# QKV weight slices 0 and 1 in row halves on two DMA queues, in a fused attention and SwiGLU kernel

## The chip, the cores and the metric

The kernel runs on one core of a Trainium2 chip. The metric is the device time of one execution in microseconds (us); the figure given is the median over runs.

## The reference

All tensors are bfloat16. One layer norm of `x` feeds two branches, and both are added to `x`: a local, dilated attention (32 heads of 18, each position sees 8 positions at distance 0, 2, ..., 14 before it) and a SwiGLU block.

```python
x = A_x                                   # (1, 2048, 576)
xn = _layernorm(x)
return x + _A_ref(xn, A_wqkv, A_wo) + _B_ref(xn, B_w_gate, B_w_up, B_w_down)

def _A_ref(x, wqkv, wo):                  # wqkv (576, 1728), wo (576, 576)
    q, k, v = split_heads(x @ wqkv)       # H = 32, Dh = 18
    idx = pos[:, None] - 2 * arange(8)    # masked where idx < 0
    attn = softmax(q . k[idx] * Dh ** -0.5)
    return merge_heads(attn . v[idx]) @ wo

def _B_ref(x, w_gate, w_up, w_down):      # (576, 4608), (576, 4608), (4608, 576)
    return (silu(x @ w_gate) * (x @ w_up)) @ w_down
```

## The kernel before

The 2048 positions are cut into 16 "rows" of 128: position `16 p + r` lies in partition `p` of row `r`, so each partition of an x load reads consecutive bytes. The width of 576 makes five slices of the contraction: `kt` 0 to 3 of 128 each, and `kt` 4 of 64, which is laid in both halves of the partitions.

**Loads at the start (lines 144 to 165).** A DMA is issued by an engine's queue: `nc.sync` is SyncE's, `nc.scalar` ScalarE's. `load_x(eng, j)` brings one x row (144 KB) into `xc_b[0]`, `load_w(eng, kt)` one slice of the QKV weights (432 KB; slice 4 as two transfers of 64 partitions and 108 KB). The order is written out by hand: ScalarE issues x row 0 and slice 1; SyncE issues x row 1, slice 0, slice 2, x row 2, slice 3, slice 4, x row 3, and then x rows 4 to 15 in three transfers of four rows (576 KB each). The x buffers lie in the tile `wd`, the QKV weights in the tile `hT`, both of which get their real contents later; in the profile their transfers are called so. Every transfer tells of its landing through one of eight counters, taken in turn over both queues.

**Start of the computation (lines 477 to 523).** TensorE first runs products of constants (`warm_pe`). Row 0 is centred on VectorE as soon as its statistics are there, transposed on TensorE (`transp_pe`, L262), copied by ScalarE into `xcT` (L268, in the tile `PP`) in three pieces, and multiplied with the QKV slices in the order 0, 1, 2 (`p_whole`, L301, four products of 432 columns for each slice); the division by the standard deviation follows when the result is copied out (`p_evac`). Row 1 is normalized meanwhile (L240, its 64 columns of padding on GpSimd, L243), transposed between the products of slice 2, and its products with slice 0 stand ahead of row 0's with slice 3 and slice 4 (`p_row0_rest`). The weights' loads are waited for by the first product that reads them.

**The rest.** Rows 1 to 15 go through `p_row`, in products of 64 by 128 that run in pairs; from row 5 on x is transposed by DMA. The statistics of two rows (`ln_stats`, L214) are taken about four rows ahead; those of rows 8 and 9 while TensorE is at row 4. Keys and values go through `stage` buffers in `hT` into a ring of rows, and to DRAM (`store`, L384) for later. Then four passes over 512 positions each follow: nine chunks of gate and up products (`g_pair`, L600) and the down and output products (`d_half`, L629). The chunk weights (`load_gu`) of chunk `it + 2` are issued when chunk `it` is done. VectorE and ScalarE do the attention beside TensorE, in portions that `dve.pump` lets out. In the first pass, after chunk 0, the values of the last four rows are written to DRAM in three pieces (`store(2, 3, 3)`).

Of the kernel before, what the change touches and what calls it, by code (L numbers as in the profile page):

```python
# [17 lines left out]
P = 128  # L18
H, DH, W, DIL = 32, 18, 8, 2
D = H * DH  # L20
# [50 lines left out]
def kernel(  # L71
# [11 lines left out]
    nc = tc.nc  # L83
# [6 lines left out]
    x_v = A_x.rearrange("b (p r) d -> p (b r) d", r=R)  # L90
# [31 lines left out]
    wdf = wd[:].rearrange("p f j -> p (f j)")  # L122
    XC, XN = RT * D, RT * DPAD
    xc_b = [wdf[:, i * XC:(i + 1) * XC].rearrange("p (r d) -> p r d", d=D) for i in range(4)]
# [4 lines left out]
    wqkv = hTf[:, 0:12 * D].rearrange("p (k j) -> p k j", j=3 * D)  # L129
# [14 lines left out]
    def load_x(eng, j):  # L144
        eng.dma_start(xc_b[0][:, j:j + 1, :], x_v[:, j:j + 1, :])  # L145

    def load_w(eng, kt):
        if kt < 4:
            eng.dma_start(wqkv[:, kt, :], A_wqkv[kt * P:(kt + 1) * P, :])
        else:  # L150
            for i in range(2):
                eng.dma_start(wqkvr[64 * i:64 * i + 64, :], A_wqkv[4 * P:D, 2 * G * i:2 * G * (i + 1)])

    load_x(nc.scalar, 0)
    load_x(nc.sync, 1)
    load_w(nc.scalar, 1)
    load_w(nc.sync, 0)
    make_identity(nc, ident[:])
    load_w(nc.sync, 2)
    load_x(nc.sync, 2)  # L160
    load_w(nc.sync, 3)
    load_w(nc.sync, 4)
    load_x(nc.sync, 3)
    for c in range(1, 4):
        nc.sync.dma_start(xc_b[c], x_v[:, 4 * c:4 * c + 4, :])
    nc.scalar.activation(warm[:], eps_t[:], ACT.Sqrt)

    wp = ps.tile([P, 512], f32, name="warm_ps", tag="ps")
# [10 lines left out]
    def load_gu(it):  # L179
        ch, slot = it % NCH, it % NSLOT  # L180
        fc = slice(ch * FC * P, (ch + 1) * FC * P)
        nc.sync.dma_start(gu[:, slot, 0:4, :], B_w_gate[0:512, fc].rearrange("(kt kp) n -> kp kt n", kp=P))
        nc.sync.dma_start(gu[:, slot, 4:8, :], B_w_up[0:512, fc].rearrange("(kt kp) n -> kp kt n", kp=P))
        nc.sync.dma_start(gu[0:64, slot, 8, :], B_w_gate[512:576, fc])
        nc.sync.dma_start(gu[64:128, slot, 8, :], B_w_up[512:576, fc])

    def load_wo(d):
        k, row = divmod(d * H, P)
        for lo in (row, row + 64) if k == KT - 1 else (row,):
            nc.sync.dma_start(wo[lo:lo + H, k, :], A_wo.rearrange("(h d) j -> d h j", d=DH)[d])  # L190

    def load_wd(ch):
        nc.sync.dma_start(wd[:, ch * FC:(ch + 1) * FC, :],
                          B_w_down[ch * FC * P:(ch + 1) * FC * P, :].rearrange("(f p) j -> p f j", p=P))
# [185 lines left out]
    def store(m, c, parts=1):  # L380
        st = stage[(2 * c + m - 1) % 4].rearrange("p r d -> p (r d)")
        n = XC // parts
        for i in range(0, XC, n):
            nc.sync.dma_start(kv_d[m - 1, c - 1, :, i:i + n], st[:, i:i + n])  # L384
# [197 lines left out]
    def g_pair(tt, ch, p):  # L582


        slot = (tt * NCH + ch) % NSLOT
        tok = slice(tt * TT, (tt + 1) * TT)
        js = (2 * p, 2 * p + 1)
        fence = {}
        for j in js:
            ring_ps[j] = [new_ps("g_ps") for b in range(2)]  # L590
        for swap in range(2):
            for j in js:
                fc = slice(j * P, (j + 1) * P)
                kts = (0, 1, 2, 3) if swap else (0, 4, 1, 2, 3)
                for kt in kts:
                    for half in range(2):
                        b = half ^ swap
                        rows = slice(64 * half, 64 * half + 64)
                        k = 8 if kt == 4 else 4 * b + kt
                        mm = nc.tensor.matmul(ring_ps[j][b][:], gu[rows, slot, k, fc], xnT[rows, kt, tok],  # L600
                                              start=(swap == 0 and kt == 0), stop=(swap == 1 and kt == 3))
                        if swap == 0 and kt == 3 and half == 1:
                            fence[j] = fence_after(mm)
                        if swap and kt == 0 and half == 0:
                            fence_before(mm, fence[j])

    def g_evac(ch, j):
        t = ring_ps[j]
        sg = tmp.tile([P, TT], bf16, name="sg", tag="sg", bufs=3)
        uc = tmp.tile([P, TT], bf16, name="uc", tag="uc", bufs=3)  # L610
        nc.scalar.activation(sg[:], t[0][:], ACT.Silu)  # L611
        nc.scalar.copy(uc[:], t[1][:])  # L612
        nc.vector.tensor_tensor(hT[:, ch * FC + j, :], sg[:], uc[:], op=ALU.mult)  # L613

    def d_half(tt, sub, swap, t, fence):


        r = RT * tt + sub
        tiles = [(hT[:, f, sub * P:(sub + 1) * P], wd[:, f, :]) for f in range(NF)]
        tiles += [(oT[:, k, r * P:(r + 1) * P], wo[:, k, :]) for k in range(KT - swap)]  # L620
        if r == R - 1:
            tiles.insert(NF, (ident, xr[:, sub, :]))
        if not swap:
            t[sub] = [new_ps("d_ps") for h in range(2)]
        for n, (a, w) in enumerate(tiles):
            for half in range(2):
                rows = slice(64 * half, 64 * half + 64)
                h = half ^ swap
                mm = nc.tensor.matmul(t[sub][h][:, 0:HALF], a[rows], w[rows, h * HALF:(h + 1) * HALF],  # L629
                                      start=(swap == 0 and n == 0), stop=(swap == 1 and n == len(tiles) - 1))  # L630
                if not swap and n == len(tiles) - 1 and half == 1:
                    fence[sub] = fence_after(mm)
                if swap and n == 0 and half == 0:
                    fence_before(mm, fence[sub])

    def d_out(r, sub, t):
        ot = tmp.tile([P, D], bf16, name="ot", tag="ot", bufs=3)
        for h in range(2):
            cols = slice(h * HALF, (h + 1) * HALF)
            if r < R - 1:  # L640
                nc.vector.tensor_tensor(ot[:, cols], t[h][:, 0:HALF], xr[:, sub, cols], op=ALU.add)  # L641
                continue
            (nc.scalar.copy, nc.vector.tensor_copy)[h](ot[:, cols], t[h][:, 0:HALF])  # L643
        nc.sync.dma_start(out_v[:, r, :], ot[:])

    for tt in range(NTT):
        for ch in range(NCH):
            it = tt * NCH + ch
            for p in range(2):
                g_pair(tt, ch, p)  # L650
                for j in (2 * p, 2 * p + 1):
                    g_evac(ch, j)
                    if it % NCH < NCH - 1 or p == 0:
                        dve.pump(1.4)
            if ch == NCH - 1:
                dve.drain(lambda: chains[0] > tt)
                for r in range(RT * tt, RT * tt + RT):
                    nc.sync.dma_start_transpose(oT[:, :, r * P:(r + 1) * P], QOP[:, r, :])
                for i in (0, 2):
                    nc.sync.dma_start(xr[:, i:i + 2, :], x_v[:, RT * tt + i:RT * tt + i + 2, :])  # L660
            if it + NSLOT < NTT * NCH:
                load_gu(it + NSLOT)
            if tt == 0:
                if 1 <= ch <= 7:
                    load_wd(ch - 1)
                if ch in (3, 4):
                    load_wd(11 - ch)
                for _ in range(3 if ch in (1, 2) else 2):
                    if wo_order:
                        load_wo(wo_order.pop(0))  # L670
                if ch == 0:
                    store(2, 3, 3)
            if ch == 1 and tt < NTT - 1:
                chain(tt + 1)
        for sub in range(0, RT, 2):
            t, fence = {}, {}
            for swap in range(2):
                for i in (sub, sub + 1):
                    d_half(tt, i, swap, t, fence)
                    if swap:  # L680
                        dve.pump(12.5 if i == sub else 4.0)
                        d_out(RT * tt + i, i, t[i])
# [30 lines left out]
```

## Time and profile before

| | |
|---|---|
| median of 3 runs | 503.36 us (503.14 to 503.4) |
| the profiled execution | 503.32 us, its span 501.5 us |
| PE (TensorE) busy | 496.8 us, 99% |
| DVE (VectorE) / ACT (ScalarE) / POOL (GpSimd) busy | 329.0 / 200.6 / 2.6 us |
| moved by DMA | 75.42 MB, mean 150 GB/s |
| ScalarE's DMA queue (q10) | 288 packets, 0.59 MB |
| SyncE's DMA queue (q1) | 76840 packets, 73.98 MB |
| clock granted to TensorE | 1.00 |

Times in the profile are microseconds from the start of the span. An engine's name with a q (SPq, ACTq) is its issuing of instructions, PEld is TensorE's loading of the operand that stays in the array. `out<-in` names the tiles written and read; `xcount` is the number of instructions in a line, and what stands in brackets is the idle time ahead of it and what ended it. Ends of products are modelled, so a busy TensorE need not be at its peak.

### The profile page before, as it was taken

Reading aid. Unit: us, or ns where it says so; the run is one execution under the profiler, and the core shown is the slowest. Engines: PE = TensorE matmul, PEld = TensorE weight load, DVE = VectorE, ACT = ScalarE, POOL = GpSimd, SP = SyncE. Lnnn points to the kernel's source line nnn. Section 1 sums busy time; section 2 is a strip of 40 time slices with the busy share of each in tenths; the row PEclk is TensorE's granted clock in tenths of the full one; section 3 lists DMA queues with packets and bytes.
Section 4 is the critical chain, followed back from the end, with each engine's and each line's share of the span. In section 5 each row is a group of like instructions: output and inputs, shape, how many; then the busy total and the mean of one; then the engine's idle time right before and its main releaser. Section 6 shows DMA issues by size and latency. Waiting matters only on the chain.

```text
span 501.5 us, 13267 instructions
## 1 busy us (share of the span) xinstructions
PE 496.8 (99%) x5795; PEld 282.8 (56%) x5795; DVE 329.0 (66%) x478; ACT 200.6 (40%) x415; POOL 2.6 (1%) x9
## 2 busy tenths in 40 slices
PE   8999999999999999999999999999999999999997
PEld 4555544444677644444777544445777444446775
DVE  5889597998999698999897139995980222221001
ACT  4756657645300255544300445557000454553000
POOL 2000000000000000000000000000000000000000
PEclk9999999999999999999999999999999999999999
DMA  8689989898731045535631154453700335442200
GB/s 322 164 207 228 320 268 294 260 318 272 186 114 61 25 147 185 190 112 174 166 106 47 30 182 154 131 189 110 181 26 14 106 110 177 159 126 39 76 14 25
DMA packets 77186, 75.42 MB, mean 150 GB/s; under 512 B 22708, under 2 KB 72528, under 8 KB 77128
## 3 DMA queue, kind: packets, MB, share of 16 engines
q1 hardware_dynamic: 76840, 73.98, 49.2%
q8 instruction: 45, 0.74, 0.7%
q10 hardware_dynamic: 288, 0.59, 0.3%
q14 instruction: 13, 0.11, 0.1%
HBM read 58.76 MB, written 5.90 MB: 129 GB/s over the span
## 4 chain that ended last, share of the span: by engine, by line
PE 98%; DMA 1%; DVE 0%; SPq 0%; issue 0%
PE g_ps L600 56%; PE d_ps L629 32%; PE qkv_ps L301 11%; DMA hT<-in_A_wqkv_dram 1%; DVE ot L643 0%; PE pt L283 0%; SPq L145 0%; PE pt L262 0%; PE warm_ps L262 0%
## 5 line engine op out<-in xcount | busy, mean ns | idle before, releaser
L600 PE MATMUL g_ps<-xnT,gu 64*128 64x512 bf16 x2592 | 280.4, 376 | 0.0
L600 PEld LDWEIGHTS <-gu 64*128 64x128 bf16 x2592 | 126.1, 94 | 152.9
L611 ACT ACTIVATE sg<-g_ps 128x512 bf16<-128x512 f32 x144 | 87.3, 606 | 156.6 <-PE g_ps L600 156.6
L629 PE MATMUL d_ps<-wd,hT 64*128 64x288 bf16 x2304 | 146.4, 283 | 0.0
L629 PEld LDWEIGHTS <-hT 64*128 64x128 bf16 x2304 | 112.2, 94 | 29.7
L613 DVE TENSOR_TENSOR hT<-sg,uc 128x512 bf16<-128x512 bf16 x144 | 60.0, 419 | 93.9 <-ACT uc L612 93.8
L612 ACT CAST uc<-g_ps 128x512 bf16<-128x512 f32 x144 | 85.2, 592 | 0.0
L414 DVE TENSOR_REDUCE PP<-PP 128x64 f32<-128x1152 bf16 x64 | 84.9, 1346 | 0.4
L301 PE MATMUL qkv_ps<-hT,xnT 64*128 64x432 bf16 (+1 forms) x536 | 50.1, 343 | 0.0
L409 DVE TENSOR_TENSOR PP<-QO,Kr 128x2304 bf16<-128x2304 bf16 (+1 forms) x35 | 43.5, 1249 | 7.0 <-DMA Kr<-hT 6.8
L641 DVE TENSOR_TENSOR ot<-d_ps,xr 128x288 bf16<-128x288 f32 x30 | 12.3, 450 | 51.1 <-PE d_ps L629 51.1
L441 DVE TENSOR_TENSOR PP<-Vr,A 128x2304 bf16<-128x2304 bf16 (+1 forms) x35 | 43.2, 1250 | 0.4
L301 PEld LDWEIGHTS <-xnT 64*128 64x128 bf16 (+1 forms) x536 | 25.9, 94 | 22.5 <-ACT xnT L287 0.2
L446 DVE TENSOR_TENSOR PP<-PP 128x2304 bf16<-128x2304 bf16 x24 | 32.5, 1353 | 0.3
L611 ACT ACT_TABLE_LOAD x5 | 6.4, 1283 | 47.2 <-PE g_ps L600 47.2
L629 PE MATMUL d_ps<-wo,xnT 64*128 64x288 bf16 x288 | 22.9, 283 | 0.0
L363 ACT CAST hT<-qkv_ps 128x288 bf16<-128x288 f32 (+2 forms) x58 | 21.1, 427 | 0.5 <-ACT hT L363 0.5
L434 ACT ACTIVATE PP<-PP 128x1024 f32<-128x1024 f32 x4 | 4.2, 1056 | 31.2 <-DVE PP L430 31.2
L629 PEld LDWEIGHTS <-xnT 64*128 64x128 bf16 x288 | 14.0, 94 | 3.6
L643 ACT CAST ot<-d_ps 128x288 bf16<-128x288 f32 x1 | 0.4, 399 | 38.8 <-PE d_ps L629 38.8
L363 ACT CAST QO<-qkv_ps 128x432 bf16<-128x432 f32 (+1 forms) x30 | 12.3, 409 | 7.4 <-PE qkv_ps L301 7.4
L214 DVE BATCH_NORM_STATS2 stats<-wd 128x6 f32<-128x288 bf16 x32 | 12.9, 444 | 2.8 <-DMA wd<-in_A_x_dram 2.6
(53 smaller groups left out, 89.4 us busy)
## 6 DMA issues: line engine op xcount, KB each, us to landing
gu<-in_B_w_gate_dram SPq DMA_DIRECT2D x36, 512.0 KB, 3.9
gu<-in_B_w_up_dram SPq DMA_DIRECT2D x36, 512.0 KB, 5.2
wd<-in_B_w_down_dram SPq DMA_DIRECT2D x9, 576.0 KB, 6.4
kv_d<-hT SPq DMA_DIRECT2D x5, 576.0 KB, 6.0
gu<-in_B_w_gate_dram SPq DMA_DIRECT2D x36, 64.0 KB, 5.0
gu<-in_B_w_up_dram SPq DMA_DIRECT2D x36, 64.0 KB, 4.6
xr<-in_A_x_dram SPq DMA_DIRECT2D x8, 288.0 KB, 3.9
out_dram<-ot SPq DMA_DIRECT2D x16, 144.0 KB, 1.8
```

What stands on the lines that cost most here:

```text
L214: nc.vector.bn_stats(sums[r][:, k, :], xc[:, j, k * HALF:(k + 1) * HALF])
L301: return nc.tensor.matmul(t[g][:, 0:G], xT_of(r)[rows, kt, :], w_at(g, kt, rows), start=start, stop=stop)
L363: (nc.vector.tensor_copy if n in dve else nc.scalar.copy)(*parts[n])
L409: nc.vector.tensor_tensor(prod[:, a:b], QO[:, RT * tt + a:RT * tt + b, :], Kr[:, s:s + b - a, :], op=ALU.mult)
L414: nc.vector.tensor_reduce(L[:, w, rs], prod[:, rs].rearrange("p r (h d) -> p r h d", d=DH), axis=AX.X, op=ALU.add)
L441: nc.vector.tensor_tensor(dst[:, a:b], Vr[:, s:s + b - a, :].rearrange("p r (d h) -> p r d h", h=H), A[:, w, a:b].unsqueeze(2).to_broadcas ...
L446: nc.vector.tensor_tensor(dst, acc, pv, op=ALU.add)
L600: mm = nc.tensor.matmul(ring_ps[j][b][:], gu[rows, slot, k, fc], xnT[rows, kt, tok], start=(swap == 0 and kt == 0), stop=(swap == 1 and kt ...
L611: nc.scalar.activation(sg[:], t[0][:], ACT.Silu)
L612: nc.scalar.copy(uc[:], t[1][:])
L613: nc.vector.tensor_tensor(hT[:, ch * FC + j, :], sg[:], uc[:], op=ALU.mult)
L629: mm = nc.tensor.matmul(t[sub][h][:, 0:HALF], a[rows], w[rows, h * HALF:(h + 1) * HALF], start=(swap == 0 and n == 0), stop=(swap == 1 and ...
```

## The change

Slices 0 and 1 are each loaded as two transfers of 64 rows (216 KB): rows 0 to 63 on SyncE's queue, rows 64 to 127 on ScalarE's, slice 0 ahead of slice 1 on both. x rows 8 to 15 come in one transfer of 1152 KB instead of two of 576. The store of the last values goes out in two pieces of 288 KB instead of three of 192, so the number of transfers over the whole kernel stays what it was.

```diff
     load_x(nc.scalar, 0)
     load_x(nc.sync, 1)
-    load_w(nc.scalar, 1)
-    load_w(nc.sync, 0)
+    for kt in range(2):
+        for eng, lo in ((nc.scalar, 64), (nc.sync, 0)):
+            eng.dma_start(wqkv[lo:lo + 64, kt, :], A_wqkv[kt * P + lo:kt * P + lo + 64, :])
     make_identity(nc, ident[:])
     load_w(nc.sync, 2)
     load_x(nc.sync, 2)
     load_w(nc.sync, 3)
     load_w(nc.sync, 4)
     load_x(nc.sync, 3)
-    for c in range(1, 4):
-        nc.sync.dma_start(xc_b[c], x_v[:, 4 * c:4 * c + 4, :])
+    nc.sync.dma_start(xc_b[1], x_v[:, 4:8, :])
+    nc.sync.dma_start(wdf[:, 2 * XC:4 * XC].rearrange("p (r d) -> p r d", d=D), x_v[:, 8:16, :])
     nc.scalar.activation(warm[:], eps_t[:], ACT.Sqrt)
...
                 if ch == 0:
-                    store(2, 3, 3)
+                    store(2, 3, 2)
```

## The prediction

> **What bounds the kernel now.** I read first the chain that ended last in order of time, then the start of the timeline, then the windows of the first 13 us (transfer rate), and last the waits of SyncE's queue. The chain:
>
> ```profile
> 1.17 4.79 DMA hT<-in_A_wqkv_dram
> 5.97 0.04 issue
> 6.01 1.99 PE qkv_ps L301 x10
> ...
> 12.46 3.10 PE qkv_ps L301 x34
> ...
> 19.14 40.52 PE qkv_ps L301 x444
> 59.66 69.93 PE g_ps L600 x648
> 129.59 39.69 PE d_ps L629 x648
> ```
>
> From 6.01 us to the end of the products at 498.4 the chain never leaves TensorE, so a change to the loads can do one of two things: let TensorE start its first real product earlier than 6.01, or make it wait somewhere later. The start hangs on QKV slice 0, issued on SyncE's queue at 1.17 and landed at 5.97. What else the first product needs is in the timeline:
>
> ```profile
> 5.45 0.27 ACT L268 COPY PP<-pt 128x128 bf16<-128x128 bf16 x1 [0.28 <-PE pt L262]
> ...
> 5.77 1.80 PEld L301 LDWEIGHTS <-PP 128*128 128x128 bf16 x10
> 5.93 0.37 ACT L268 COPY PP<-pt 128x256 bf16<-128x256 bf16 x1 [0.21 <-PE pt L262]
> 6.01 1.99 PE L301 MATMUL qkv_ps<-hT,PP 128*128 128x432 bf16 x10
> ```
>
> The other operand, the transposed x row 0, is copied by 5.72 and is in the array from 5.77. So slice 0 holds TensorE for 6.01 - 5.77 = 0.24 us, and that is all that its earlier landing can give.
>
> The rates (columns: stretch, length, busy time of PE, PEld, DVE, ACT, POOL, then clock, DMA share, GB/s):
>
> ```profile
> 3.00:5.00 2.00, 1.53 (x7) 0.45 (x4) 1.15 (x4) 0.26 (x2) 0.06 (x1) 1.00 1.03 408
> 5.00:6.00 1.00, 0.63 (x5) 0.42 (x6) 1.00 (x4) 0.51 (x3) 0.53 (x1) 1.00 1.04 418
> 6.00:7.50 1.50, 1.49 (x9) 0.81 (x9) 1.33 (x6) 0.86 (x3) 0.96 (x2) 1.00 1.05 398
> 7.50:9.25 1.75, 1.75 (x14) 1.03 (x13) 1.02 (x4) 0.74 (x2) 0.40 (x1) 1.00 1.08 314
> 9.25:13.00 3.75, 3.75 (x46) 1.91 (x45) 3.05 (x10) 2.49 (x7) 0.00 (x0) 1.00 1.02 410
> ```
>
> From 3 us on the transfer engines are full at about 410 GB/s, except from 7.5 to 9.25, where they moved 314. What moved there is the last QKV slice, two transfers of 64 partitions each (L152, 0.22 MB together), and x row 3. That is the only row of this trace on 64-partition transfers, and the change makes four more of them.
>
> **The change part by part.** The sum is made against the profiled execution, 503.32 us: a span of 501.5 and 1.8 around it. The median of the runs is 503.36, so a difference can be laid on either.
>
> *Order of slices 0 and 1.* Before, slice 1 stood on ScalarE's queue and slice 0 on SyncE's, 0.44 MB each, and they shared the engines: the trace has them landed at 5.68 and 5.97. After, each queue has a half of slice 0 ahead of a half of slice 1, so slice 0 is whole after half of these bytes. The x rows 0 and 1 landed at 3.75 and 3.93; the two slices took 5.97 - 3.93 = 2.04 us more, half of it gives about 4.95, and at the poorest rate of the table (314 instead of 410) 5.27. Both are ahead of 5.72, so TensorE starts on its other operand: at 5.77, plus one more wait, since a product now needs two landings. The chain shows 0.04 from a landing to the product; I take 0.05, between nothing and 0.10, and a start at 5.82: a gain of 0.19 us (bounds 0.14 to 0.24).
>
> *Does it carry on?* Products of the first row run every 0.182 us. Slice 1 is due at 5.82 + 4 x 0.182 = 6.55; the copy of L268 that it needs ends at 6.30. Slice 2 is due at 6.01 + 8 x 0.182 = 7.47 before and 7.28 after; in the trace it landed at 7.14, with 0.04 to the product 7.18. Its margin shrinks from 0.29 to 0.10. Slice 3 landed at 8.84, due at 9.31 before and 9.12 after; slice 4 at 9.58, due at 10.14 and 9.95. The row 1 operand is normalized by 7.44 (VectorE) and 7.90 (its padding, GpSimd) and wanted from 7.64 and 8.17. So slice 2 is the next thing to be late, if the halves travel slower than whole slices.
>
> *Rate of the halves.* By the page of before, 1.75 us at 314 instead of 410 GB/s lose 1.75 x 96/410 = 0.41 us on 0.22 MB of lone halves, 1.86 us per MB. Not all of the new halves are alone: while ScalarE's queue sends rows 64 to 127, SyncE's sends rows 0 to 63. The two queues end apart, though: up to 4.75 us ScalarE's had moved 0.57 of its 0.59 MB, SyncE's only 0.45, so the last 0.14 MB of slice 1 go on SyncE's queue with no partner. Priced by the row of the lone halves that is 0.14 x 1.86 = 0.26 us by which everything behind comes later. The bounds are 0 (the halves pair perfectly, or the 314 came from the short rows of slice 4 and x row 3) and 0.88 x 1.86 = 1.65 us (each half as slow as a lone one). I take 0.26, since the traffic up to the point where ScalarE's queue runs empty is over all 128 partitions as in the stretch of 408. Slice 1 then lands at 6.23, in time. Slice 2 is ready at 7.18 + 0.26 = 7.44 against 7.28: TensorE waits 0.16 of its 0.19 again. Slice 3 is ready at 9.14 against 9.28, slice 4 at 9.88 against 10.11: nothing more.
>
> [...]
>
> *Issues.* An issue takes about 0.44 us on SyncE and 0.46 on ScalarE. ScalarE gets one more, which moves its table load from 1.63 to 2.09 and the end of its warm-up from 3.13 to 3.59; its next work is at 4.88, so 1.29 us of idle time cover it (0.46 without). SyncE's queue gets one more issue ahead of slice 2, and the trace shows each transfer held until the one eight places before it has landed:
>
> ```profile
> SPq L165 <- DMA hT<-in_A_wqkv_dram: 1.4, 2, 0.8
> SPq L183 <- DMA hT<-in_A_wqkv_dram: 0.9, 1, 0.9
> ```
>
> Two transfers more move these pairs: slice 3 now waits for x row 0 (3.75), slice 4 for x row 1 (3.93) and a half of slice 0 (about 4.9), x row 3 for the other half, x rows 4 to 7 for a half of slice 1 (about 6.0 instead of 5.70). Slice 3 is issued at about 3.8 instead of 2.62, slice 4 from 4.3 instead of 3.11. By then 1.76 MB are issued and some 0.6 moved, so over 2.5 us of traffic stand ahead of slice 3: no gap in the transfers, no cost. If that cover were gone, slice 3 would land up to 1.2 us later, 0.7 past its due time.
>
> *x rows 8 to 15 in one, the last store in two.* The merged load takes one issue of 0.33 to 0.43 us away ahead of the first gate weights, due at 59 us and landed by 18. Rows 8 to 11 are seen only when rows 12 to 15 have landed too, at 14.3 instead of 12.8; the statistics of row 8 run at 23.96 (the ninth pair of L214), so 9.7 us cover it. The store in two pieces instead of three saves an issue of 0.46 at 70.8 us, after which SyncE idles from 72.15 to 75.23. Nothing waits for either: zero. The gate and up loads of later chunks are issued after TensorE's own progress and move with it.
>
> The sum: -0.19 + 0.16 = -0.03 us, 503.33.
>
> **The rivals.** (a) *The halves pair at full rate*: slice 2 is still at 7.18, the whole 0.19 stays, 503.17; at most 0.24, 503.12. For it: 408 GB/s with two queues on different slices, and short rows as another reading of the 314. Against: the 0.14 MB without a partner.
> (b) *Slower: the halves get in each other's way all along.* Then each travels like a lone half, slice 2 comes 1.65 us later, at 8.83 against 7.28, and the time is 503.36 - 0.19 + 1.55 = 504.7; slice 0 would land at about 5.8, just in time for its start. It decides from a loss of 0.29 us on (slice 2 past 7.47), and passes 0.2% (1.0 us, about what a measurement of this kernel can tell from no change) from 1.29 on, that is when the four halves move at under about 255 GB/s. For it: the 314 row. Against: that row is two halves one behind the other on one queue, here the queues hold opposite halves. [...]
> (c) *The change doesn't do what it says*: a queue runs so far ahead that slice 0 is whole no earlier than 5.97. The start stays at 6.01, slice 2 at 7.44 is in time for 7.47, and the time is 503.36. Against: in the trace the queues drifted apart by 0.12 MB of 0.59 only.
>
> **How the numbers follow.** Forecast, a loss of 0.1 to 0.5 us on the halves: 0.48. (a): 0.28. (b) with a loss of 0.5 to 1.29: 0.10, over that 0.06. (c): 0.04. Only the far part of (b) is slower by over 0.2%; faster by over 0.2% needs 1.0 us where 0.24 is to be had, so 0.02 stands there for what the trace doesn't show, and 0.02 likewise on the slow side: 0.02, 0.90 and 0.08. The predicted time is 503.33. The range goes down to (a) less the spread of the runs (503.14 against 503.36): 502.9, and up into (b) at a loss of about 0.9 us: 504.0.
>
> **What would show it.** In the profile after: the first chain piece of L301 at about 5.8 with x row 0's copy or transposes ahead of it, not a DMA; an idle time of TensorE of 0.1 to 0.3 us ahead of the ninth product, released by the QKV load; a rate between 4.7 and 6 us under 410 GB/s. A start at 6.0 makes (c) right; a rate near 410 and no wait at slice 2 (a); a wait of over half a microsecond there (b). I am wrong altogether if TensorE waits anywhere after 13 us, or if the span moves by more than the start and the waits ahead of 13 us explain.

## The result: slower by 0.36%

The changed kernel takes 504.99 us (median; 504.56 to 505.79), the kernel before beside it 503.38 us (503.14 to 503.5). The ratio of the means is 1.0036 with a 95% interval of 1.0024 to 1.0048. That is outside the forecast's range (502.9 to 504.0) and close to what rival (b) gave, 504.7. The profiled execution took 505.02 us with a span of 503.1, so 1.6 us more than the span of before, at a granted clock of 1.0.

### The profile page after: what moved, and what is told of

Its sections match the earlier page's. It is cut to its first block, busy times and chain, and to the rows that moved or that the text cites. A ratio compares the mean times of both kernels' runs of the same rounds, so it can differ in the third digit from the quotient of the medians.

```text
span 503.1 us, 13268 instructions
## 1 busy us (share of the span) xinstructions
PE 497.9 (99%) x5795; PEld 414.5 (82%) x5795; DVE 329.1 (65%) x478; ACT 200.6 (40%) x415; POOL 2.6 (1%) x9
## 4 chain that ended last, share of the span: by engine, by line
PE 98%; DMA 1%; SPq 0%; ACT 0%; issue 0%
PE g_ps L601 56%; PE d_ps L630 32%; PE qkv_ps L302 10%; DMA hT<-in_A_wqkv_dram 1%; SPq L158 0%; PE pt L284 0%; ACT ot L644 0%; SPq L145 0%; PE pt L263 0%; PE warm_ps L263 0%
## 5 line engine op out<-in xcount | busy, mean ns | idle before, releaser
L601 PEld LDWEIGHTS <-gu 64*128 64x128 bf16 x2592 | 208.1, 94 | 71.1
L630 PE MATMUL d_ps<-wd,hT 64*128 64x288 bf16 x2304 | 148.4, 283 | 0.0
L630 PEld LDWEIGHTS <-hT 64*128 64x128 bf16 x2304 | 142.5, 94 | 0.4
L302 PEld LDWEIGHTS <-xnT 64*128 64x128 bf16 (+1 forms) x536 | 42.6, 94 | 6.0 <-ACT xnT L288 0.2
L630 PE MATMUL d_ps<-wo,xnT 64*128 64x288 bf16 x288 | 24.9, 283 | 0.0
L630 PEld LDWEIGHTS <-xnT 64*128 64x128 bf16 x288 | 18.9, 94 | 0.0
```

The costliest lines, as they stand in the source:

```text
L302: return nc.tensor.matmul(t[g][:, 0:G], xT_of(r)[rows, kt, :], w_at(g, kt, rows), start=start, stop=stop)
```

## The profile after

The chain of waits of the changed kernel (start, length, what):

```profile
1.18 0.57 SPq L158
1.75 0.04 issue
1.79 6.21 DMA hT<-in_A_wqkv_dram
8.00 0.14 issue
8.14 0.89 PE qkv_ps L302 x4
9.03 0.04 issue
9.06 0.52 PE qkv_ps L302 x2
...
20.81 40.51 PE qkv_ps L302 x443
61.32 69.93 PE g_ps L601 x648
131.25 39.69 PE d_ps L630 x648
```

The chain comes onto TensorE at 8.14 and not at 6.01, and by way of the half of slice 1 that SyncE issued at 1.79 and that landed at 8.00. From there on the pieces are as long as before (40.51 against 40.52, 69.93, 39.69), so nearly everything was lost ahead of them: the gate products begin at 61.32 instead of 59.66, 1.66 later.

The start in the timeline of the changed kernel (start, busy time, instruction; in brackets the idle time ahead of it and what ended that):

```profile
4.41 0.82 DVE L215 BATCH_NORM_STATS2 stats<-wd 128x6 f32<-128x288 bf16 x2 [3.23 <-DMA wd<-in_A_x_dram]
...
6.08 0.27 ACT L269 COPY PP<-pt 128x128 bf16<-128x128 bf16 x1 [0.28 <-PE pt L263]
...
6.90 0.89 PE L302 MATMUL qkv_ps<-hT,PP 128*128 128x432 bf16 x4 [0.38 <-DMA hT<-in_A_wqkv_dram]
...
8.14 1.45 PE L302 MATMUL qkv_ps<-hT,PP 128*128 128x432 bf16 x6 [0.35 <-DMA hT<-in_A_wqkv_dram]
```

Three readings. The first product starts at 6.90, 0.89 later than before. Products follow each other every 0.182, so the fourth starts at 7.45, and the next, which needs slice 1, would at 7.63; it comes at 8.14: 0.51 lost. The pair for slice 2 then comes 0.20 late (9.06 against 8.68 + 0.18). The sum, 0.89 + 0.51 + 0.20 = 1.60, is the whole difference of the spans; the 0.06 by which the gate products are later still is gone again at the very end. And x row 0 was late as well: its statistics start at 4.41 and its first copy ends at 6.35 (5.72 before). The statistics in the timeline of before:

```profile
3.78 0.82 DVE L214 BATCH_NORM_STATS2 stats<-wd 128x6 f32<-128x288 bf16 x2 [2.60 <-DMA wd<-in_A_x_dram]
```

The windows of the first 13 us (the columns as in the prediction, GB/s last):

```profile
3.00:5.00 2.00, 2.00 (x7) 0.59 (x4) 0.59 (x2) 0.86 (x2) 0.00 (x0) 1.00 0.99 254
5.00:6.00 1.00, 0.47 (x3) 0.10 (x1) 0.93 (x5) 0.29 (x1) 0.43 (x1) 1.00 1.04 321
6.00:7.50 1.50, 1.04 (x9) 0.55 (x8) 1.43 (x7) 1.07 (x4) 0.49 (x2) 1.00 1.01 267
7.50:9.25 1.75, 1.37 (x8) 0.52 (x7) 0.53 (x3) 0.13 (x1) 1.02 (x2) 1.00 1.04 384
```

Where before moved 408, 418 and 398 GB/s, after moved 254, 321 and 267, with the transfer engines just as fully busy (0.99 to 1.04 in the column before the rate). Once the halves are through, at 8.0 us, the rate is back (398 from 8.0 to 9.25). Over the whole stretch from 3 to 8 us it is 281 GB/s against 403, which is 1.5 us of traffic less. In the packet records a row of 3456 bytes took 252 ns on average between 2.5 and 4 us and 194 between 4 and 7, where it took 140 and 138 before; the median from 4 to 7 is 184 against 135, so it is the usual packet that became slower, and not a few. Some long ones came on top: twelve of 0.49 to 1.09 us between 3 and 8, where before had none over 0.33. The landings follow: x rows 0 and 1 at 4.38 and 4.15 (3.75 and 3.93 before), slice 0's halves at 6.46 (ScalarE's) and 6.77 (SyncE's), slice 1's at 7.82 and 8.00, slice 2 at 9.02 (7.14 before).

## The experiments

Unless something else is said, an edit is made to two lines of the kernel before, `load_w(nc.scalar, 1)` and `load_w(nc.sync, 0)`, and a time is a median, with the median of the kernel before on the same chip beside it. A ratio is that of the means, with its 95% interval.

### One part at a time

**Halves only.** The changed kernel's four halves; x rows and store as before.

```diff
-    load_w(nc.scalar, 1)
-    load_w(nc.sync, 0)
+    for kt in range(2):
+        for eng, lo in ((nc.scalar, 64), (nc.sync, 0)):
+            eng.dma_start(wqkv[lo:lo + 64, kt, :], A_wqkv[kt * P + lo:kt * P + lo + 64, :])
```

> Only slices 0 and 1 in row halves; the x loads and the last store stay as before. If the row halves carry the loss (theory R): about 505.0 us, slice 2 ready near 9.0 us and TensorE waiting for slices 0, 1 and 2 as in the profile after. If the merged x load or the store has a part in it (theory M): nearer to 503.4, by as much as e2 is slower.

504.94 us against 503.24, ratio 1.0038 (1.0023 to 1.0053). The rate from 3 to 8 us is 283 GB/s and the median packet from 4 to 7 took 199 ns. Only three packets took over 0.48 us, so the loss does not need the long packets.

**Merged x load and store only.**

```diff
-    for c in range(1, 4):
-        nc.sync.dma_start(xc_b[c], x_v[:, 4 * c:4 * c + 4, :])
+    nc.sync.dma_start(xc_b[1], x_v[:, 4:8, :])
+    nc.sync.dma_start(wdf[:, 2 * XC:4 * XC].rearrange("p (r d) -> p r d", d=D), x_v[:, 8:16, :])
...
-                    store(2, 3, 3)
+                    store(2, 3, 2)
```

> Only the x rows 8 to 15 in one transfer and the store in two pieces; slices 0 and 1 whole as before. R: 503.4, no difference, first product at 6.0 us. M: slower by up to 1.6.

503.34 against 503.24, ratio 1.0002 (0.9993 to 1.0012). The two together settle it: the loss is in the halves, and the other two edits cost nothing that can be measured.

### The same order without the row halves

**Column halves.** Slices 0 and 1 still go half on each queue, but each half holds all 128 partitions and 864 of the 1728 columns (with the merged x load and the store).

```diff
+    for kt in range(2):
+        for eng, lo in ((nc.scalar, 864), (nc.sync, 0)):
+            eng.dma_start(wqkv[:, kt, lo:lo + 864], A_wqkv[kt * P:(kt + 1) * P, lo:lo + 864])
```

> As the changed kernel, but slices 0 and 1 are cut by columns: each queue loads 864 of the 1728 columns of all 128 partitions, slice 0 ahead of slice 1 on both. As many transfers, issues and bytes on each queue as in the changed kernel, each over all partitions. R (it is the 64 partitions that are slow): the engines stay near 400 GB/s from 3 to 7 us, slice 0 is whole at about 5.0, the first product comes at 5.8 and the time is 503.1 to 503.4. Rival Q (two more transfers, one more issue on each queue and slices shared by two queues are what costs): as the changed kernel, 504.5 to 505.5, under 330 GB/s from 3 to 7 us.

504.67 against 503.24, ratio 1.0028 (1.0016 to 1.004). Its windows:

```profile
3.00:5.00 2.00, 2.00 (x7) 0.59 (x4) 1.08 (x4) 0.67 (x3) 0.00 (x0) 1.00 1.07 387
5.00:6.00 1.00, 0.98 (x8) 0.52 (x7) 1.00 (x4) 0.51 (x2) 0.58 (x1) 1.00 1.09 361
```

Its timeline:

```profile
5.91 0.90 PE L302 MATMUL qkv_ps<-hT,PP 128*128 128x432 bf16 x4
7.42 0.53 PE L302 MATMUL qkv_ps<-hT,PP 128*128 128x432 bf16 x2 [0.61 <-DMA hT<-in_A_wqkv_dram]
8.96 0.97 PE L302 MATMUL qkv_ps<-hT,PP 128*128 128x432 bf16 x4 [1.01 <-DMA hT<-in_A_wqkv_dram]
```

The rate came back for the most part (387 GB/s where the row halves had 254 and before 408), slice 0 was whole at 4.92 (the prediction's step had 4.95), and the first product started at 5.91. So the order does what it was read to do, and with as many transfers, issues and bytes on each queue the rate was lost to the row halves. But the time did not come back: slice 1 landed at 7.38 and 8.91. In the packet records 13 of the 16 transfer engines had finished their shares of the later piece by 6.0; the rest came after single packets of 936 to 1352 ns, where 74 were usual. The changed kernel has long packets too, but here the usual packet is not slower (72 ns from 4 to 7 us, and 135 for slice 2's rows of 3456 bytes), so this is another loss in the main. It is taken up below.

**Slices swapped.** `load_w(nc.scalar, 0)` and `load_w(nc.sync, 1)`.

> Before with one edit: slice 0 on ScalarE's queue and slice 1 on SyncE's, both whole. In the trace of before ScalarE's slice landed 0.29 us ahead of SyncE's. If the prediction's step on the start holds (the other operand is ready at 5.77), slice 0 lands at about 5.68, the first product comes at 5.77 to 5.8, and the whole 0.2 us stays to the end: 503.15. If something else holds the start or takes the gain back, 503.4.

503.57 against 503.24, ratio 1.0006 (0.9996 to 1.0015). In its profile SyncE's queue ran ahead (slice 1 landed at 5.79, slice 0 on ScalarE's at 6.34), where in the profile of before ScalarE's did (slice 1 on it at 5.68, slice 0 on SyncE's at 5.97). So which queue is ahead is not fixed.

### Other doses and other rows

**Only slice 0 in halves**, slice 1 whole behind it on ScalarE's queue.

```diff
+    nc.scalar.dma_start(wqkv[64:P, 0, :], A_wqkv[64:P, :])
+    nc.sync.dma_start(wqkv[0:64, 0, :], A_wqkv[0:64, :])
     load_w(nc.scalar, 1)
-    load_w(nc.sync, 0)
```

> Only slice 0 in row halves, one on each queue; slice 1 whole behind it on ScalarE's. Half of the dose. R: half of the loss of rate, slice 0 at 5.5 to 6.5 and slice 1 about 0.8 us earlier than with four halves, 503.8 to 504.4. Q: as with four halves or nearer to before, since only one more transfer is issued.

507.64 against 503.46, ratio 1.0079 (1.0064 to 1.0094): half the halves cost more than twice as much, against the expectation. Two things in its profile: the lower half of slice 0, on SyncE's queue, landed only at 7.96, 2.76 behind the upper one, while ScalarE's queue went on with the whole slice 1 beside it; and behind the long wait TensorE's clock was halved. Why the transfer engines were only 0.78 busy from 3 to 5 us, at 202 GB/s, is open.

```profile
9.00:10.00 1.00, 0.58 (x3) 0.32 (x3) 0.00 (x0) 0.00 (x0) 0.00 (x0) 0.89 1.08 292
10.00:11.00 1.00, 1.00 (x4) 0.44 (x3) 0.00 (x0) 0.00 (x0) 0.00 (x0) 0.50 1.07 327
```

These are two windows of 1 us; the clock, third from the end, is at 0.50 from 10 to 13 us. So the time of such a kernel cannot be read as a cost of transfers alone.

**Rows 32 to 95** on SyncE's queue, 0 to 31 and 96 to 127 on ScalarE's.

```diff
+    for kt in range(2):
+        for eng, lo, hi in ((nc.sync, 32, 96), (nc.scalar, 0, 32), (nc.scalar, 96, P)):
+            eng.dma_start(wqkv[lo:hi, kt, :], A_wqkv[kt * P + lo:kt * P + hi, :])
```

> As the halves alone, but cut at other rows: rows 32 to 95 of slices 0 and 1 on SyncE's queue, rows 0 to 31 and 96 to 127 on ScalarE's. Two more transfers than with four halves. R: a transfer of rows 32 to 95 moves as a whole one does, the two of 32 rows are as slow as lone halves; less loss than e1, 503.6 to 504.5. Q: at least as slow as e1, 505 or more.

508.27 against 503.46, ratio 1.0085 (1.0056 to 1.0113); the smaller loss that was expected did not come. The profile is of the fastest of four executions (506.03). The two more transfers meant that slice 1's last piece was issued only at 3.90 (1.79 in the changed kernel) and landed at 8.96, and TensorE waited 1.75 us for it, so the time does not price rows 32 to 95. The rate did not come back either: 278 GB/s from 3 to 5 us and 290 from 5 to 6. From 4 to 5.5 us the packets of rows 32 to 95 took 196 ns (median) and those of the pieces of 32 rows beside them 206, so rows 32 to 95 were not fast in this company.

**Halves crossed**: ScalarE's queue has the upper half of slice 1 first, SyncE's the lower half of slice 0, so that the two halves of one slice are not issued side by side.

```diff
+    for i in range(2):
+        for eng, lo, kt in ((nc.scalar, 64, 1 - i), (nc.sync, 0, i)):
+            eng.dma_start(wqkv[lo:lo + 64, kt, :], A_wqkv[kt * P + lo:kt * P + lo + 64, :])
```

> The four halves with ScalarE's two exchanged: rows 0 to 63 of slice 0, then 1 on SyncE's queue; rows 64 to 127 of slice 1, then 0 on ScalarE's. At any time the two queues read different slices, and the halves still complement each other. P and N: as slow as e1, 504.9, with packets of about 200 ns (slice 0 whole even later). H: packets of about 137 ns and a time near that of before, 503.3 to 503.7.

507.05 against 503.31, ratio 1.0072 (1.0055 to 1.0089). The rates of its windows are the changed kernel's (255 GB/s from 3 to 5 us and 283 from 5 to 6, where that had 254 and 321), so it is not the two queues' reading one slice that is slow. Slice 0 is whole only at 7.78, and a clock of 0.50 from 8 to 11 us adds to the loss.

### The rate by itself

**Loads in the quiet end of the kernel**, into a buffer that is no longer read.

> The kernel before with seven groups of extra loads into the dead key ring in the last 40 us, where nearly nothing else moves: (1) two whole slices, one on each queue; (2) the same two slices in row halves, as the change has them; (3) one whole slice on SyncE's queue; (4) rows 0 to 63 of two slices, one behind the other; (5) rows 32 to 95 of two slices; (6) two slices in column halves, one half on each queue; (7) rows 0 to 63, then 64 to 127 of one slice. Theory R (which partitions a transfer covers sets its rate): (1), (3), (5), (6) at about 400 GB/s, (4) and (7) at about 200, (2) in between, 200 to 330; the packets of 3456 bytes take about 137 ns in (1) and (3), 200 to 270 in (2) and (4). Theory Q (the number of transfers, or two queues on one slice): (3) fast, (4), (5) and (7) alike, and (2) and (6) alike. The time of the run is of no interest.

The first packets after a quiet stretch took 300 to 700 ns and more, whatever their rows, and only then some 135, and that start-up covered most of several groups. Three stretches are free of it:

```profile
469.25:469.75 0.50, 0.50 (x14) 0.40 (x10) 0.00 (x0) 0.00 (x0) 0.00 (x0) 1.00 1.03 408
470.50:471.75 1.25, 1.25 (x26) 1.00 (x22) 0.00 (x0) 0.00 (x0) 0.00 (x0) 1.00 1.02 268
477.00:477.75 0.75, 0.75 (x16) 0.60 (x14) 0.00 (x0) 0.00 (x0) 0.00 (x0) 1.00 1.02 230
```

The first is a whole slice alone on SyncE's queue, the second halves on both queues (group 2), the third rows 0 to 63 alone (group 4). But group 4 had begun with half a microsecond at 373 (476.5 to 477.0), so groups this short are no safe measure of a steady rate.

**The same with a lead-in**: each group stands behind column halves that start the traffic. The groups of 0.88 MB:

```diff
...
+        if slot[0] == 1:                      # whole slices, one on each queue
+            load(a, 1, 1)
+            load(s, 0, 0)
+        elif slot[0] == 3:                    # as the change does it
+            for kt in range(2):
+                load(a, kt, kt, 64, P)
+                load(s, kt, kt, 0, 64)
+        elif slot[0] == 5:                    # rows 0 to 63 on both queues
+            for kt in range(2):
+                load(a, kt, kt, 0, 64)
+                load(s, 2 + kt, 2 + kt, 0, 64)
+        elif slot[0] == 7:                    # rows 32 to 95 on both queues
+            for kt in range(2):
+                load(a, kt, kt, 32, 96)
+                load(s, 2 + kt, 2 + kt, 32, 96)
```

> The kernel before with four groups of 0.88 MB of extra loads into the dead key ring in the last 40 us, each behind 0.44 MB of whole-height loads on both queues that take the slow start after a quiet time: (1) two whole slices, one on each queue; (2) rows 0 to 63 of slices 0 and 1 on SyncE's queue beside rows 64 to 127 on ScalarE's, as the change; (3) rows 0 to 63 on both queues, of four slices; (4) rows 32 to 95 on both queues, of four slices. Theory P (a transfer is held by the share of the partitions that the traffic of the moment covers): (1) and (4) at about 400 GB/s with packets of 137 ns, (3) at about 200 with packets of 270, (2) at 220 to 330, since the queues drift. Rival H (what is slow is two queues reading one slice): (2) slow, (3) and (4) as fast as (1). Rival N (any transfer of 64 rows is slow, wherever its rows lie): (2), (3) and (4) alike.

This too is one execution. The first group did not come as planned: its two queues moved at different times. SyncE's share of it, whole-height loads alone, moved at 391 GB/s from 468.0 to 469.5. The windows of the second, third and fourth group:

```profile
473.50:476.00 2.50, 2.50 (x46) 1.99 (x42) 0.82 (x2) 0.00 (x0) 0.00 (x0) 1.00 0.99 267
483.00:486.00 3.00, 3.00 (x54) 2.36 (x52) 0.00 (x0) 0.00 (x0) 0.00 (x0) 1.00 1.06 215
493.50:495.00 1.50, 1.50 (x30) 1.19 (x26) 0.82 (x2) 0.00 (x0) 0.00 (x0) 1.00 0.98 354
```

Nearly all packets here are of 64-row transfers, with the engines about equally busy. Rows 0 to 63 on both queues: 215 GB/s, the median packet 269 ns. Rows 32 to 95 on both: 354, and 135 ns, the time of a whole slice's packets. So in these groups it is not the number of rows that costs, and not that a slice is cut, but which partitions the traffic reaches. The opposite halves of the change, on two queues, get 267, and 244 from 474.5 to 476.5, when the group's faster beginning is over: 14 to 24% more than one half alone, far from the 354. This is the forecast's disputed quantity, measured alone: the halves hardly pair.

What makes rows 0 to 63 slower than rows 32 to 95 no run here shows, and why opposite halves do not pair is only partly seen. In the packet records of the changed kernel the queues are out of step: between 3.0 and 4.5 us ScalarE's started 0.23 MB and SyncE's 0.12. But from 5.0 to 5.5 both started 0.08, and the rate was still 318. What holds them back then is open.

### The order without halves, four ways

**Both slices on SyncE's queue, one behind the other.**

```diff
-    load_w(nc.scalar, 1)
     load_w(nc.sync, 0)
+    load_w(nc.sync, 1)
```

> Before with one edit: slices 0 and 1 whole, both on SyncE's queue, slice 0 first; ScalarE's queue has x row 0 alone. The order that the change wanted, without halves. Theory R and the prediction's step on the start: slice 0 lands at about 5.0, slice 1 at 6.0, the first product comes at about 5.8 and the time is 503.1, 0.1 to 0.25 below before. Theory Q (shared queues are not the cost, but the start is held by something else): 503.3, as before.

504.64 against 503.46, ratio 1.0022 (1.0012 to 1.0032). The timeline, of the slowest of ten executions (505.71):

```profile
5.82 0.97 PE L301 MATMUL qkv_ps<-hT,PP 128*128 128x432 bf16 x4
8.09 0.89 PE L301 MATMUL qkv_ps<-hT,PP 128*128 128x432 bf16 x4 [1.30 <-DMA hT<-in_A_wqkv_dram]
9.53 0.53 PE L301 MATMUL qkv_ps<-hT,PP 128*128 128x432 bf16 x2 [0.55 <-DMA hT<-in_A_wqkv_dram]
```

The start is the predicted 5.82 to the digit, with slice 0 landed at 4.80. But slice 1, of which 11 of 16 shares were there by 5.84, was whole only at 8.05, after packets of up to 1196 ns, six of them over 900, between 4.0 and 6.6 us. The median packet from 4 to 7 us still took 135.

**The same kernel in another execution.**

> e6 once more, to see its loads a second time. If the packets of about 1 us between 4 and 7 us belong to this order of loads, they are there again and slice 1 is whole at 7 or later, with most of the engines done before 6. If they were an accident of one execution, slice 1 lands at about 6.0 and the first nine products run without a wait of over 0.2 us, near 503.2.

504.38 against 503.23, one execution: packets of 834 to 1318 ns between 4.2 and 6 us again, the start at 5.66, waits of 0.39 and 0.36 after it. So the delayed packets were no accident of one execution. They are not confined to this order: the changed kernel's profile has one of 1.09 us, and that of the halves of slice 0 one of 1.04.

**Slices 0 and 1 on SyncE's queue, slice 2 on ScalarE's.**

```diff
-    load_w(nc.scalar, 1)
     load_w(nc.sync, 0)
+    load_w(nc.scalar, 2)
+    load_w(nc.sync, 1)
...
-    load_w(nc.sync, 2)
```

> As e6 (slices 0 and 1 whole and one behind the other on SyncE's queue), with slice 2 moved to ScalarE's, so that both queues are busy with whole slices, as in before. If e6 was slow because a single queue was left to the engines, so that each delayed packet held everything behind it: no packets of a microsecond, slice 0 at about 5.7, 503.1 to 503.5. If it was slow because slice 0 alone was read: the same, since slice 2 is read beside it. If it is the order itself: as e6, 504.6.

503.9 against 503.31, ratio 1.0014 (1.0005 to 1.0024). No packet took over 560 ns, but slice 0 shares the engines with slice 2 and lands at 6.43, so the first product starts at 6.47 and the order's point is gone.

**Both x rows on ScalarE's queue, slice 0 first on SyncE's.**

```diff
-    load_x(nc.sync, 1)
-    load_w(nc.scalar, 1)
     load_w(nc.sync, 0)
+    load_x(nc.scalar, 1)
+    load_w(nc.scalar, 1)
```

> Whole slices, two busy queues, and slice 0 first in another way: ScalarE's queue has x rows 0 and 1 and slice 1, SyncE's slice 0 and then slice 2 and the rest. If the start step of the prediction holds and e6 was slow only for its delayed packets: slice 0 at about 4.9, x row 0 at 3.9 (it now shares the engines with slice 0), first product at 5.8 to 6.0, slice 1 at 6.0, 503.1 to 503.4. If putting slice 0 ahead is itself what brings the delayed packets: 504 to 505, with a spread of over 1 us between runs.

506.07 against 503.23, ratio 1.0049 (1.0036 to 1.0062). The timeline:

```profile
5.03 0.82 DVE L214 BATCH_NORM_STATS2 stats<-wd 128x6 f32<-128x288 bf16 x2 [3.85 <-DMA wd<-in_A_x_dram]
...
6.44 0.71 PE L262 MATMUL pt<-ident,wd 128*128 128x128 bf16 x5 [1.76 <-DVE wd L251]
7.03 3.54 PE L301 MATMUL qkv_ps<-hT,PP 128*128 128x432 bf16 x10
```

Slice 0 came early (4.82), with 395 GB/s moved from 3 to 5 us, and now x row 0 was late: 5.01 instead of 3.75. Its packets are 1152 bytes, slice 0's 3456, and in the records the queues come near to taking turns by packets: from 3.0 to 4.5 us SyncE's started 133 large packets (0.46 MB) and ScalarE's 104 (0.12 MB). The queue of small packets got a small share, 0.12 of 0.58 MB. After the idle 1.76 us the ten products took 3.54 us, at a clock of 0.50 to 0.66, where they take 1.99.

### Slices left on their queues, and TensorE kept busy

**Each slice cut in two where it stands**: lower, then upper half, slice 1 on ScalarE's queue and slice 0 on SyncE's as before.

```diff
+    for lo in (0, 64):
+        for eng, kt in ((nc.scalar, 1), (nc.sync, 0)):
+            eng.dma_start(wqkv[lo:lo + 64, kt, :], A_wqkv[kt * P + lo:kt * P + lo + 64, :])
```

> Before, with each of slices 0 and 1 cut into rows 0 to 63 and 64 to 127 on its own queue: ScalarE's has slice 1, SyncE's slice 0, both the lower rows first. Now both queues write the same half of the partitions at the same time. P: the worst of the halves: about 200 GB/s while the halves run, packets of 250 ns and more, 505 to 507. H: as before, 503.3. N: as e1, 504.9.

508.01 against 503.31, ratio 1.0086 (1.0061 to 1.0111). With the order untouched and only the cut added, the rate is 252 GB/s from 3 to 5 us and 259 from 5 to 6 (408 and 418 before): the cut alone loses it. The timeline:

```profile
8.36 3.43 PE L302 MATMUL qkv_ps<-hT,PP 128*128 128x432 bf16 x10 [1.96 <-DMA hT<-in_A_wqkv_dram]
```

The ten products take 3.43 instead of 1.99 us, at a granted clock of 0.50 from 8 to 11 us.

**The same with eight products of constants** (`warm_pe(8, 0)`) put ahead of row 0's first product.

> e11 (both queues write the same half of the partitions) with one addition: eight products of constants, 512 columns each, between row 0's transposes and its first product, in the time in which TensorE waits there for slice 0. If e11's products at half clock between 8 and 11.3 us come from that idle time: the granted clock stays at 1.0, the first ten products take 1.8 to 2.0 us instead of 3.43, and the time falls by about 1.5 us against e11, to 506.0 to 506.8 with less spread. If the clock has another cause: as e11, 506 to 509.

506.57 against 503.23, ratio 1.0066 (1.0051 to 1.0082). The timeline:

```profile
6.31 1.91 PE L175 MATMUL warm_ps<-const-bfloat16-1.0 128*128 128x512 bf16 x8
9.12 1.99 PE L302 MATMUL qkv_ps<-hT,PP 128*128 128x432 bf16 x10 [0.90 <-DMA hT<-in_A_wqkv_dram]
```

With the wait filled the clock stays at 1.00 and the ten products take 1.99, though slice 0 landed even later (its first product at 9.12 against 8.36). The loss over the kernel before goes from 4.70 to 3.34 us by the medians, 1.4 less, though the four runs of each overlap (506.0 to 509.04, 506.0 to 507.41); by the products in the profiles, 3.43 against 1.99, the clock cost the same 1.4. In the changed kernel itself this plays no part; its clock is 1.00 in every window, and its waits are short and broken up by products.

None of these versions beats the kernel before; the slices swapped and the merged x load are level with it.

## Why the prediction was wrong, step by step

**What bounds the kernel** was right: all that was lost was lost ahead of 13 us, at the first product and at the two waits after it, and these three make up the 1.6 us.

**The step that failed is "rate of the halves".** It took a loss of 0.26 us; measured on the same thing, the landing of slice 2, it was 9.02 - 7.14 = 1.88 (1.59 in the profile of the halves only). About 1.5 of it is the traffic missing from 3 to 8 us, at 281 GB/s for 403; the rest is the last two of slice 2's 16 shares, since fourteen of them came 1.53 later than before. The reason it gave was that up to the point where ScalarE's queue runs empty the traffic "is over all 128 partitions as in the stretch of 408". The traffic was, and the rate was not: 254, 321 and 267 GB/s while both queues had halves to send, and 244 to 267 in the group measured by itself. The prediction gave the price that it took for a lone half to the 0.14 MB without a partner only. The same price for all 0.88 MB gives 1.65, its upper bound, and even that was short of 1.88.

That this bound came so near is partly luck, for the row of 314 was misread. It holds 0.55 MB, of which slice 4 and x row 3 are 0.36; the rest is the end of slice 3 and the first of x rows 4 to 7. Cut finer, it is 370 GB/s from 7.5 to 8.0, 263 from 8.0 to 8.5, and 311 from 8.5 to 9.25, when all but 9 of the 128 packets of slice 4 had started. So it is no price of lone halves, and part of its dip has another cause, which no run here tells. Measured by themselves, lone halves moved at 215.

**The start step** had its arithmetic right and its rate wrong. "Whole after half of the bytes" held where the rate held: slice 0 at 4.92 in column halves, 4.80 on one queue, against 4.95 predicted, and starts of 5.91, 5.82 and 5.66 against 5.82. In the changed kernel slice 0 took until 6.77. Two smaller things were missed in it. x row 0, taken as fixed at 3.75, moves beside the halves on the same transfer engines and came at 4.38, so even with an early slice 0 the first product could not have started before 6.35. And a product that needs two landings started 0.13 to 0.14 us after the last one, not 0.05.

**"Does it carry on?"** was right in its method. It named slice 2 as the next to be late; with the larger loss slice 1 was late already (0.51) and slice 2 only by 0.20 more. Slice 3 was in time, with nothing to spare (landed at 10.87, its product at 10.91), and the second piece of slice 4 made its first product 0.08 late.

**Issues, the merged load and the store** were right at zero. Slice 3 was issued at 4.40 (about 3.8 was said) and the second piece of slice 4 at 6.48, when the half of slice 0 eight places before it had landed; that piece's 0.08 is all that could be laid on the issues. The merged load and the store alone gave 1.0002.

**The rivals.** (b) was right in its mechanism, and its 504.7 is near the 504.99; its price came from the misread row. It had the loss in one wait at slice 2 and a start at 5.82, where the start itself took more than half of it. Its threshold, under about 255 GB/s, is where the stretch from 3 to 5 us lies (254). The argument against it, that the queues hold opposite halves, was the same unproved pairing. Halves that only took turns would give, as an estimate from the group of rows 0 to 63, its 215 GB/s; 244 to 267 were measured, so they paired a little. (a) fell: no stretch reached 410 while halves moved. (c) came true in part: slice 0 was whole only at 6.77, and the queues had drifted apart, with 89 packets of halves started on ScalarE's and 57 on SyncE's by 5.0 us. How much of slice 0's delay is this drift and how much the rate no run separates; (c)'s time, 503.36, had the halves lose 0.26 only. No rival had a start as late as 6.90.

## What to carry to other kernels

Price a transfer by the partitions that it reaches (here rows 0 to 63 at 215 GB/s and rows 32 to 95 at 354), and give two complementary halves on two queues no credit for pairing (244 to 267 here) unless a row of the trace shows them paired. If a load is to land sooner, all else in flight with it is part of the step: here x rows, which were ahead in the queues, came later too (4.38 and 4.15 instead of 3.75 and 3.93). If the first product waits, look at the granted clock behind the wait before the wait is taken for the whole loss: with the slices cut in place, 1.4 of the 4.70 us came from a clock of 0.50.

## What the runs showed of the hardware that was not expected

- Sixty-four rows are not slow as such: rows 32 to 95 moved at 354 GB/s and rows 0 to 63 at 215, on the same two queues, in one execution. Beside pieces of 32 rows, at the kernel's start, rows 32 to 95 were slow too (196 ns a packet instead of 135).
- With both x rows on ScalarE's queue, the two queues started nearly as many packets each from 3.0 to 4.5 us (133 and 104), so the bytes went with the packet size: 0.46 MB against 0.12 with packets of 3456 and 1152 bytes.
- A wait of TensorE of 1.4 to 2 us at the start was followed by a clock of 0.50 for about 3 us in the profiles of four kernels (halves of slice 0 alone, crossed, cut in place, both x rows on ScalarE's queue), and not in that of rows 32 to 95, with a wait of 1.75; filling it with products of constants, tried for the slices cut in place, kept the clock at 1.00 and was worth 1.4 us.
- With both slices one behind the other on one queue, and with column halves on two, single packets took 0.8 to 1.35 us and held back a few engines' shares of a slice, while the median packet stayed as before. The four row halves had single long packets as well, and a slower median. In the versions with whole slices on both queues the longest from 3 to 8 us took 0.56. Why is open.
